# Where the second batch's keys and values are pooled in a fused attention and two-layer MLP kernel

## The chip, the cores and the metric

The kernel runs on one core of a Trainium2 chip. The metric is the device time of one execution in microseconds (us), where lower is better. Single executions are compared by the median of several; a profiled execution gives the trace. The engines are named as the profile names them: PE (TensorE matmuls), PEld (its weight loads), ACT (ScalarE), DVE (VectorE), POOL (GpSimd) and SP (SyncE), which issues all the transfers here.

## What is computed

Three stages follow each other. The attention stage takes 8 batches of 8 heads with 576 tokens and 64 channels; keys and values are averaged over groups of 8 tokens, so each head has 72 of each.

```python
k_p = k.reshape(B, H, Sp, pool, D).mean(axis=3)
v_p = v.reshape(B, H, Sp, pool, D).mean(axis=3)
scores = scale * np.matmul(q, k_p.transpose(0, 1, 3, 2))
attn = softmax(scores)                    # over the 72 pooled keys
x = np.matmul(attn, v_p)                  # then 4608 tokens x 512
```

The second stage is `x = g(x @ w_in) @ w_out` with 2048 hidden units, where g is a ratio of two polynomials. The third is `(sigmoid(x @ w_gate) * (x @ w_val)) @ w_out` with 1536 hidden units. All is float32 in and out.

## The kernel before

Every large product is made of three matmuls in a split form (`mm3`, L484): each operand is held as a high part, which is its rounded copy, and a low part, which is the rest. Weights are brought into that form by `conv1a` (two ACT instructions for each matrix, L92 and L94), `conv1b` (one on DVE, L100, and one on POOL, L102) and `conv2` (L117 on ACT, and L118 on DVE for `w_in` and on POOL for `w_out`).

The main loop (L771) runs over 144 steps n: 9 blocks of 512 tokens times 16 slices of 128 hidden units. Step n issues, in this order: `g1` (12 matmuls into a PSUM tile h), `run(on_pe, n, 0)`, `rational1` (ACT L526 to L528, then DVE L529 to L531), `run(off_pe, n, 0)`, `split_g` of the step before (ACT L511, POOL L514), `rational2` (ACT L537, L539), `run(off_pe, n, 2)`, `gap` (L100 and L102 of the weights that ACT treated in the step before), `rational3` (DVE L543 to L545, after which h is free), `g2` of step n - 3 (12 matmuls), `run(on_pe, n, 1)`, `run(off_pe, n, 1)`, and in the first 16 steps `weights_a` (L117, L118, then L92 and L94, then two transfers of raw weights). Steps -8 to -1 are a lead-in that pools the first batch and makes the first block of x. Each engine takes its instructions strictly in this order.

The attention of a tile of up to 128 tokens is spread over steps by a table: `put(step, rank, pe, rest, ...)` (L444) names the step and in which of the calls above a part runs. `scores` (L360 on PE, then L371 and L373 on DVE) stands three steps ahead of the tile's own step, `exponential` (L379) and `normalise` (L386 to L389 on DVE, L390 on POOL) two ahead, `a_transpose` (L397 on PE, L401 on ACT) at the step, and `attend` (L415 on PE, L421 and L422) one behind it. Tile 4, the last of the first batch, belongs to step 2; tile 5, the first of the second batch, to step 5; tile 6 to step 8.

A batch's keys come in 5 chunks and its values in 5. `pool_k` (L319) is one DVE reduction for a chunk, and `place_k` (L328) copies the whole pooled result on ACT into `kbd`, the operand that `scores` needs. `pool_v` is three POOL additions for a chunk (L336 twice, L337), and `mask_v` (L351) makes on POOL the operand `vm` that `attend` needs. They are wrapped in a generator that does nothing at its first call and the work at its second. So an entry with rest 2 and pe 1 is entered at `run(off_pe, n, 2)` and does its work at `run(on_pe, n, 1)`, after `rational3`; an entry with pe 1 and rest 1 works at `run(off_pe, n, 1)`.

The raw chunks of q, k and v are loaded in the order in which the table uses them. The first 14 go to tiles that later hold weights, the next three to a ring of three tiles, five more to other idle tiles, and from then on a load is issued into the ring whenever a ring tile has been used (`done`, L303). SP issues all loads in program order, so a load that must wait for its tile holds up those behind it.

Of the kernel before, what the change touches and what calls it, by code (L numbers as in the profile page):

```python
# [35 lines left out]
def attention_moe_glu_kernel(ctx: ExitStack, tc: tile.TileContext, q, k, v, w_in, w_out, ca, cb, w_gate, w_val, w_out2, out):  # L36
# [14 lines left out]
    NCH = (H * SP + P - 1) // P  # L51
# [179 lines left out]
    with tc.manual_schedule():  # L231
# [212 lines left out]
        def put(step, rank, pe, rest, gen, *a, use=()):  # L444
            plan.append((step, rank, len(plan), pe, rest, gen(*a), use))
# [17 lines left out]
        for b in range(1, B):  # L463
            e0, e1 = max(at[first[b - 1]], -2), at[last[b - 1]]
            for c in range(2 * NCH):
                w, f = (("k", pool_k), ("v", pool_v))[c // NCH]
                st = e0 + c * (e1 - (3 if w == "k" else 1) - e0) // (2 * NCH)
                put(st, 6, 1, 1 if st < 0 else 2, ew, f, b, c % NCH, use=[(w, b, c % NCH)])
            put(e1 - 2, 3.5, 1, 1, ew, place_k, b)
            put(e1 + (e1 > 0), 1, 0, 0, ew, mask_v, b)  # L470
        plan.sort(key=lambda x: (x[0], (0, 2, 1)[x[4]], x[1], x[2]))
        units += [u for x in plan for u in x[6]]
        lead = plan[0][0]
# [402 lines left out]
```

## Time and profile before

| what | value |
|---|---|
| median of 3 runs (lowest, highest) | 1843.52 us (1843.23, 1848.96) |
| the profiled execution, its span | 1846.18 us, 1844.4 us |
| PE, PEld busy | 1788.9 us (97%), 1556.9 us (84%) |
| DVE, ACT, POOL busy | 1144.7 us, 943.9 us, 849.4 us |

The span is that of the instructions in the trace; the 1.8 us between it and the execution's time lie around the program. Times in the trace count from the span's start. PE's share is that of the whole span, but the change touches only the first 90 us, where PE is not busy throughout, so what a change is worth there has to be read from the rows of that stretch.

### The profile page before, as it was taken

The numbers are of one execution on the slowest core, as the hardware profiler recorded it, in microseconds if no ns is written. First come the engines' busy times: TensorE is split into PE (matmuls) and PEld (weight loads), VectorE is DVE, ScalarE is ACT, GpSimd is POOL, SyncE is SP. The second block draws the span as 40 slices with busy tenths as digits, with TensorE's granted clock in tenths as the row PEclk, the third lists the DMA queues.
The fourth block names the chain that finished last, engine by engine and source line by source line (L and its number), as shares of the span: only waits on it lengthen the run. The fifth ranks groups of instructions, "written<-read, shape, count | busy, mean of one in ns | idle before, by whom it ended". The sixth has DMA issues, their size and how long they took to land.

```text
span 1844.4 us, 25043 instructions
## 1 busy us (share of the span) xinstructions
PE 1788.9 (97%) x8936; PEld 1556.9 (84%) x8936; DVE 1144.7 (62%) x1786; ACT 943.9 (51%) x1763; POOL 849.4 (46%) x839
## 2 busy tenths in 40 slices
PE   6689999999999999999999999999999999999999
PEld 5577887888778887888878998998998998998997
DVE  6999887888788888888777343343343343343341
ACT  5897767676777777767776222222222222222221
POOL 5776545463564556535552244244244244244241
PEclk9799999999999999999999999999999999999999
DMA  8454444533544444434455763763763763763660
GB/s 277 140 189 148 142 147 152 186 138 129 190 172 143 136 175 152 160 117 166 160 200 180 232 203 107 238 203 107 239 204 106 239 203 106 239 204 105 205 204 36
DMA packets 123116, 312.55 MB, mean 169 GB/s; under 512 B 11504, under 2 KB 43248, under 8 KB 122992
## 3 DMA queue, kind: packets, MB, share of 16 engines
q1 hardware_dynamic: 122992, 310.95, 50.8%
q8 instruction: 71, 1.16, 0.3%
q14 instruction: 53, 0.43, 0.1%
HBM read 257.95 MB, written 52.95 MB: 169 GB/s over the span
## 4 chain that ended last, share of the span: by engine, by line
PE 75%; DVE 8%; POOL 6%; ACT 4%; issue 4%; DMA 2%; SPq 0%; POOLq 0%; ACTq 0%
PE h L486 14%; PE h L488 14%; PE h L487 14%; PE acc L486 5%; PE acc L488 4%; PE acc L487 4%; PE psx L415 3%; PE accA L723 3%; PE accA L724 3%; PE h L723 3%; PE h L724 3%; PE accA L722 3%; PE h L722 3%; DVE u L529 1%; DVE y L531 1%
## 5 line engine op out<-in xcount | busy, mean ns | idle before, releaser
L659 DVE TENSOR_TENSOR t<-h,t 128x384 f32<-128x384 f32 x360 | 200.8, 558 | 388.6 <-ACT t L667 277.6
L514 POOL TENSOR_TENSOR g<-y,g 128x512 fp32r<-128x512 f32 x144 | 188.7, 1310 | 280.6 <-ACT g L511 223.8
L712 POOL TENSOR_TENSOR t<-t 128x384 f32<-128x384 f32 x72 | 84.6, 1175 | 449.3 <-issue 253.7
L486 PE MATMUL h<-xs,wi 128*128 128x512 f32 x576 | 230.7, 400 | 3.4 <-DVE y L545 1.9
L486 PE MATMUL acc<-g,wo 128*128 128x512 f32 x576 | 232.4, 403 | 0.0
L488 PE MATMUL acc<-g,wo 128*128 128x512 f32 x576 | 225.2, 391 | 1.4 <-POOL g L514 1.4
L488 PE MATMUL h<-xs,wi 128*128 128x512 f32 x576 | 226.2, 393 | 0.3 <-DVE xs L422 0.3
L487 PE MATMUL h<-xs,wi 128*128 128x512 f32 x576 | 225.9, 392 | 0.0
L487 PE MATMUL acc<-g,wo 128*128 128x512 f32 x576 | 224.5, 390 | 0.0
L488 PE MATMUL h<-xS,wq 128*128 128x384 f32 x576 | 193.0, 335 | 0.0
L486 PE MATMUL h<-xS,wq 128*128 128x384 f32 x576 | 192.9, 335 | 0.0
L487 PE MATMUL h<-xS,wq 128*128 128x384 f32 x576 | 192.7, 334 | 0.0
L529 DVE SCALAR_TENSOR_TENSOR u<-s,coef,u 128x512 f32<-128x512 f32 x144 | 135.9, 944 | 67.4 <-ACT u L527 67.0
L543 DVE SCALAR_TENSOR_TENSOR y<-y,coef,h 128x512 f32<-128x512 f32 x144 | 107.2, 744 | 68.9 <-ACT h L539 67.6
L486 PE MATMUL h<-xA,wq 128*128 128x384 f32 x432 | 149.3, 346 | 0.1
L526 ACT ACTIVATE s<-h 128x512 f32<-128x512 f32 x144 | 85.2, 592 | 122.6 <-PE h L488 122.3
L488 PE MATMUL h<-xA,wq 128*128 128x384 f32 x432 | 144.7, 335 | 0.0
L487 PE MATMUL h<-xA,wq 128*128 128x384 f32 x432 | 144.6, 335 | 0.0
L486 PEld LDWEIGHTS h<-xs,wi 128*128 128x128 f32 x576 | 109.1, 189 | 28.1 <-DVE y L545 2.8
L488 PEld LDWEIGHTS acc<-g,wo 128*128 128x128 f32 x576 | 108.1, 188 | 25.8 <-POOL g L514 1.8
L488 PEld LDWEIGHTS h<-xs,wi 128*128 128x128 f32 x576 | 109.1, 189 | 24.4 <-DVE xs L422 0.7
L486 PEld LDWEIGHTS acc<-g,wo 128*128 128x128 f32 x576 | 108.1, 188 | 24.8
(119 smaller groups left out, 4177.7 us busy)
## 6 DMA issues: line engine op xcount, KB each, us to landing
wq<-w2d SPq DMA_DIRECT2D x252, 512.0 KB, 4.4
wo<-wod SPq DMA_DIRECT2D x88, 512.0 KB, 4.0
w2d<-wq SPq DMA_DIRECT2D x36, 512.0 KB, 2.8
x2d<-o SPq DMA_DIRECT2D x36, 256.0 KB, 2.6
out_dram<-o SPq DMA_DIRECT2D x36, 256.0 KB, 2.0
raw<-in_k_dram SPq DMA_DIRECT2D x32, 256.0 KB, 2.7
raw<-in_q_dram SPq DMA_DIRECT2D x32, 256.0 KB, 2.7
raw<-in_v_dram SPq DMA_DIRECT2D x32, 256.0 KB, 2.7
```

What stands on the lines that cost most here:

```text
L486: nc.tensor.matmul(out_, wl, xh, start=start, stop=False, skip_group_check=on)
L487: nc.tensor.matmul(out_, wh, xh, start=False, stop=False, skip_group_check=on)
L488: nc.tensor.matmul(out_, wh, xl, start=False, stop=stop, skip_group_check=on)
L514: eng.tensor_tensor(out=g[:, 1], in0=y, in1=g[:, 0].bitcast(F32), op=ALU.subtract)
L526: nc.scalar.activation(s, h, AF.Square)
L529: nc.vector.scalar_tensor_tensor(out=u, in0=s, scalar=coef[:, 5:6], in1=u, op0=ALU.mult, op1=ALU.add)
L543: nc.vector.scalar_tensor_tensor(out=y, in0=y, scalar=coef[:, 0:1], in1=r, op0=ALU.add, op1=ALU.mult)
L659: nc.vector.tensor_tensor(out=out_, in0=a, in1=b, op=ALU.add)
L712: eng.tensor_tensor(out=y, in0=x, in1=y, op=ALU.mult)
L722: nc.tensor.matmul(a[t], gh, wt[:, 0], start=(f == 0), stop=False)
L723: nc.tensor.matmul(a[t], gh, wt[:, 1], start=False, stop=False)
L724: nc.tensor.matmul(a[t], gl, wt[:, 0], start=False, stop=(f == NF2 - 1))
```

## The change

Three entries of the table change, for the second batch (b = 1) alone. Its five `pool_k` stood in the lead-in's step -2 and stand in steps 0 (three) and 1 (two). Its five `pool_v` stood in steps -1 (two) and 0 (three) and stand in steps 1 (two), 2, 3 and 4. Its `place_k` moves from step 0 to step 1, and its `mask_v` from step 3 to step 5. The order of the loads follows. No instruction is added or left out. Lines behind L467 stand 3 further down in the changed file.

```diff
                 st = e0 + c * (e1 - (3 if w == "k" else 1) - e0) // (2 * NCH)
+                if b == 1:
+
+                    st = c // 3 if w == "k" else 1 + 3 * (c - NCH) // (NCH - 1)
                 put(st, 6, 1, 1 if st < 0 else 2, ew, f, b, c % NCH, use=[(w, b, c % NCH)])
-            put(e1 - 2, 3.5, 1, 1, ew, place_k, b)
-            put(e1 + (e1 > 0), 1, 0, 0, ew, mask_v, b)
+            put(1 if b == 1 else e1 - 2, 3.5, 1, 1, ew, place_k, b)
+            put(5 if b == 1 else e1 + (e1 > 0), 1, 0, 0, ew, mask_v, b)
```

On DVE, from the last instruction of `rational3` in step 0 to that in step 1, the kernel before has (L543 to L545 are `rational3`, kp is the pooled key tile, r the normaliser of tile 4):

```order
L545 SCALAR_TENSOR_TENSOR y<-h,y 128x512
L386 TENSOR_REDUCE r<-e 64x8
L388 TENSOR_SCALAR r<-r 64x8
L389 RECIPROCAL r<-r 64x8
L118 TENSOR_TENSOR wi<-wiraw,wi 128x512
L529 SCALAR_TENSOR_TENSOR u<-s,coef,u 128x512
...
L545 SCALAR_TENSOR_TENSOR y<-h,y 128x512
L118 TENSOR_TENSOR wi<-wiraw,wi 128x512
```

and the changed kernel, with its own line numbers:

```order
L548 SCALAR_TENSOR_TENSOR y<-h,y 128x512
L319 TENSOR_REDUCE kp<-raw 128x64 x2
L319 TENSOR_REDUCE kp<-raw_204 128x64
L386 TENSOR_REDUCE r<-e 64x8
...
L118 TENSOR_TENSOR wi<-wiraw,wi 128x512
L532 SCALAR_TENSOR_TENSOR u<-s,coef,u 128x512
...
L548 SCALAR_TENSOR_TENSOR y<-h,y 128x512
L319 TENSOR_REDUCE kp<-raw_206 128x64
L319 TENSOR_REDUCE kp<-raw_208 128x32
L118 TENSOR_TENSOR wi<-wiraw,wi 128x512
```

Three reductions now stand ahead of tile 4's normaliser, and two behind the last instruction of `rational3` in step 1.

On ACT, the end of step 0 and step 1 up to its weight conversion read before (L526 opens a step, L539 is the end of `rational2`, L328 is `place_k`):

```order
L539 ACTIVATE h<-s 128x512
L328 ACTIVATE kbd<-kp 64x4x72 x2
L117 ACTIVATE wi<-wiraw 128x512
...
L526 ACTIVATE s<-h 128x512
...
L539 ACTIVATE h<-s 128x512
L117 ACTIVATE wi<-wiraw 128x512
L117 ACTIVATE wo<-woraw 128x512
```

and in the changed kernel:

```order
L542 ACTIVATE h<-s 128x512
L117 ACTIVATE wi<-wiraw 128x512
...
L529 ACTIVATE s<-h 128x512
...
L542 ACTIVATE h<-s 128x512
L328 ACTIVATE kbd<-kp 64x4x72 x2
L117 ACTIVATE wi<-wiraw 128x512
L117 ACTIVATE wo<-woraw 128x512
```

`place_k` moved by one step; it reads all five chunks of kp, and everything that ACT does for the weights of step 1 and for step 2 stands behind it.

On SP, the load of tile 6's queries (the 128x512 rows of in_q) and the loads ahead of it read in the changed kernel, from the last chunk of the second batch's values on:

```order
L296 DMA raw<-in_v_dram 64x512
L291 DMA raw<-in_k_dram 128x512
L122 DMA wiraw<-in_moe_w_in_dram 128x4x256
L124 DMA woraw<-in_moe_w_out_dram 128x1024
L291 DMA raw<-in_k_dram 128x512
L122 DMA wiraw<-in_moe_w_in_dram 128x4x256
L124 DMA woraw<-in_moe_w_out_dram 128x1024
L288 DMA raw<-in_q_dram 128x512
```

Before, it was issued once `scores` of tile 5 had used a ring tile in step 2; now it is the load that follows the last `pool_v`, in step 4, and `scores` of tile 6 needs it at the end of step 5.

## Rows read from the trace of the kernel before

**Rows 1.** Busy time by stretch: span, then PE, PEld, DVE, ACT, POOL, granted clock, DMA share, GB/s
```profile
37.00:61.00 24.00, 11.77 (x50) 8.65 (x49) 20.22 (x31) 20.67 (x41) 22.50 (x26) 0.78 0.62 208
146.00:200.00 54.00, 53.38 (x261) 44.19 (x260) 47.51 (x76) 41.89 (x76) 31.30 (x34) 1.00 0.33 115
```
**Rows 2.** Waits of PE, 37 to 180 us: total, times, longest
```profile
PE pta L397 <- POOL e L390: 7.5, 1, 7.5
PE sc L360 <- ACT aT L401: 7.3, 5, 2.0
PE h L488 <- DVE xs L422: 0.3, 1, 0.3
```
**Rows 3.** Timeline of ACT, steps 0 to 6: start, duration, instruction, idle before and releaser
```profile
44.67 0.88 ACT L328 ACTIVATE kbd<-kp 64x288 f32<-64x288 f32 x2
52.39 0.60 ACT L539 ACTIVATE h<-s 128x512 f32<-128x512 f32 x1 [0.56 <-DVE y L531]
54.98 0.68 ACT L117 ACTIVATE wo<-woraw 128x512 fp32r<-128x512 f32 x1 [1.41 <-POOL wo L118]
57.80 0.57 ACT L526 ACTIVATE s<-h 128x512 f32<-128x512 f32 x1
80.83 0.63 ACT L537 ACTIVATE s<-u 128x512 f32<-128x512 f32 x1 [4.79 <-DVE u L529]
86.18 0.59 ACT L526 ACTIVATE s<-h 128x512 f32<-128x512 f32 x1
93.59 0.57 ACT L526 ACTIVATE s<-h 128x512 f32<-128x512 f32 x1
```
**Rows 4.** Timeline of DVE; then L529's line view (37 to 170) and wait (37 to 94)
```profile
33.38 2.78 DVE L319 TENSOR_REDUCE kp<-raw 128x64 f32<-128x512 f32 x5
52.21 1.59 DVE L100 TENSOR_SCALAR wiraw<-wiraw 128x512 int32<-128x512 int32 x1
56.53 0.69 DVE L545 SCALAR_TENSOR_TENSOR y<-h,y 128x512 f32<-128x512 f32 x1
70.23 2.88 DVE L100 TENSOR_SCALAR woraw<-woraw 128x512 int32<-128x512 int32 x1
76.66 4.14 DVE L529 SCALAR_TENSOR_TENSOR u<-s,coef,u 128x512 f32<-128x512 f32 x1
103.36 1.60 DVE L529 SCALAR_TENSOR_TENSOR u<-s,coef,u 128x512 f32<-128x512 f32 x1
...
L529 DVE SCALAR_TENSOR_TENSOR u<-s,coef,u x16: 741/784/4142, 41.9 to 163.7; 128x512 f32<-128x512 f32 x16
...
DVE u L529 <- ACT u L527: 4.0, 4, 1.7
```
**Rows 5.** Timeline of POOL
```profile
45.42 1.04 POOL L102 TENSOR_TENSOR woraw<-woraw 128x512 int32<-128x512 int32 x1
...
48.65 1.26 POOL L336 TENSOR_TENSOR raw<-raw 128x256 f32<-128x256 f32 x2
49.98 0.32 POOL L337 TENSOR_TENSOR vp<-raw 128x64 f32<-128x64 f32 x1
52.37 1.14 POOL L390 TENSOR_TENSOR e<-e,r 64x576 f32<-64x576 f32 x1
67.52 3.04 POOL L351 TENSOR_TENSOR vm<-vp,mask 128x256 f32<-128x256 f32 x5 [1.65 <-PE psx L415]
78.97 1.28 POOL L514 TENSOR_TENSOR g<-y,g 128x512 fp32r<-128x512 f32 x1
```
**Rows 6.** Timeline of SP, the transfer's KB and us to landing, then two rows of PE's timeline
```profile
61.20 0.33 SPq L288 DMA_DIRECT2D raw<-in_q_dram  x1
...
raw<-in_q_dram SPq DMA_DIRECT2D x1, 256.0 KB, 2.6
...
85.05 1.33 PE L360 MATMUL sc<-kbd,raw 128*128 128x144 f32 x4 [3.08 <-DVE y L545]
89.28 0.80 PE L486 MATMUL h<-xs,wi 128*128 128x512 f32 x1
```

## Prediction

> **What bounds the kernel now.** I read the page's busy shares first, then busy time by stretch, then who waited for whom on PE, and last the timelines of the four engines over steps 0 to 6. PE is busy 97% of the span, but not at its head: from 37 to 61 us, where the steps of the main loop begin, PE works 11.8 of 24.0 us while POOL works 22.5 and ACT 20.7; from 146 us on PE is busy 53.4 of 54.0 us [rows 1]. So a shift of the moment at which PE takes over is carried to the end, and nothing else in the program moves. The reader should see in PE's waits that the longest one, 7.5 us in step 2, is for L390 on POOL, the normalisation of tile 4, and that the next sort, 7.3 us in five pieces, is for `a_transpose`'s copies on ACT [rows 2]. That second sort tells who sets the pace: ACT. A step on ACT begins with L526, at 57.80, 86.18 and 93.59 for steps 2, 5 and 6, and in between ACT stands still only where a row names a releaser: 1.41 us at L117 in step 1, 4.79 us at L537 in step 4, and under 1 us where L539 waits for DVE [rows 3]. PE's 7.5 us are therefore mostly cover: g1 of step 3, behind that stall, would have met ACT's lateness at the next copy. The change has to be summed on ACT's chain, from L526 of step 0 to L526 of step 6, and the result is shifted unchanged through the later steps, in which both versions issue the same instructions.
>
> **The change, part by part.** All terms are in us against the profiled execution.
>
> *Lead-in.* Five reductions, 2.78 in all, leave DVE [rows 4]. They stood in the shade of ACT, but for the 0.3 that PE waits at its third matmul of step 0 for a DVE result [rows 2]: -0.3.
>
> *Step 0.* `place_k`, 0.88 on ACT, goes to step 1 [rows 3]: -0.9. Five `pool_v` leave POOL, 1.65 each from the first L336 to the end of L337 [rows 5]. Behind them the two L102 of the lead-in end just where L529 of step 0 begins. L529 can be held by POOL: at 103.36 it lasts 1.60 behind one POOL instruction, against a least of 0.74 [rows 4]. Between 0 and 0.9 I take +0.4. Step 1 begins 0.8 early.
>
> *The normalisation of tile 4.* Three reductions of 0.6 now stand ahead of it on DVE, so it is 1.8 late on DVE, but POOL is free when it comes: L390 moves from 52.37 [rows 5] to about 50.1, and PE's stall of 7.5 shrinks by only 2. L529 of step 1 stood three DVE instructions of 0.7 ahead of L539's 52.39, at 50.2, and DVE had waited 1.7 for ACT there [rows 3, 4], so it was ready at 48.5. With 1.8 more it is ready at 50.4, and L390 now lies there, so it takes 1.60 and not 0.75: its end moves from 50.9 to 52.0, and L539 from 52.39 to 53.5: +1.1. Without the hold it would be +0.3.
>
> *A new wait on ACT.* `place_k` in step 1 stands on ACT directly behind L539 and needs all five chunks. The last two are reduced behind L545 of that step. "In the gaps" means here, after `rational3`, and not while ACT converts weights. L545 ended at 57.22 (56.53 and 0.69), since L100 ahead of it was held by POOL for 1.59 [rows 4]; POOL still has L118 and L514 there, so I leave L545 where it is. Two chunks, 0.6 and 0.4, bring it to 58.2. ACT is done with L539 at 54.1 and waits 4.1. The least is 3.1: three DVE instructions of 0.7 behind L539 and the two chunks. The most is 5.3, if L539 stays where it was. Then `place_k` costs its 0.9 here. The 1.41 that L117 waited for POOL's L118 [rows 3] go, because POOL does L118 of step 0 at about 51.5. Step 2 begins at 57.80 + 1.1 + 4.1 + 0.9 - 1.4 = 62.5, that is **4.7 late**. What is queued behind: the weights of step 1, the copies of tile 4's transposes and so the second half of `scores` of tile 5 and g1 of step 3 on PE.
>
> *Steps 1 to 4 on POOL.* Each `pool_v` adds 1.65 to a step's L102, L102, L118 and L514 (1.0 to 1.3 each [rows 5], some 4.7 together). With ACT's steps near 8 POOL can hold that, so I carry 4.7 to step 4. The 3.04 of `mask_v` leave step 3 [rows 5]. There they held L100 for 2.88, which made r of tile 5 late, and then L529 of step 4 fell behind L390, L118 and L514 for 4.14 until 80.8 [rows 4, 5]: that was ACT's 4.79. Now r comes in time, and L529 meets one POOL instruction. I leave 0.4 of the 4.79: -4.4. Step 5 begins 0.3 late, at 86.5.
>
> *A new wait on PE.* Tile 6's queries were loaded at 61.20 and needed at 85.05 [rows 6]. Now the load waits for the last `pool_v`, in step 4. From L539 ACT needs 4.0 to the next L526 (52.39 to 57.80 less the 1.41). POOL needs from about the same moment one instruction that holds L100 (1.0), two L102 (2.1) and `pool_v` (1.65), in all 4.8, and ends 0.8 behind the L526 at 86.5. So it ends at 87.3, and with 2.6 to landing [rows 6] `scores` of tile 6 begins at 89.9, where g1 of step 6 began at 89.28. Two groups of 1.33, as the row has them at a lowered clock, make g1 up to 3.3 late. If this one wait lowers the clock less than PE's stalls did before (granted 0.78 in the first stretch [rows 1]), g1 itself is shorter and little is lost. ACT, 0.3 late by itself, then waits for h. Between 0.3 and 3.3 I take 1.5, since clock was lost there before too.
>
> `mask_v` in step 5, 3.04, and its `vm` are needed by `attend` in step 6, a step later: nothing. The other moved loads are issued at least a step ahead of use: nothing; if SP fell a step behind, the weights of step 6 would be late next.
>
> **The sum**: -0.3 - 0.9 + 0.4 (step 1) + 1.9 + 4.1 + 0.9 - 1.4 (step 2; 1.1 late though it began 0.8 early) - 4.4 (step 5), then 1.5 in place of the 0.3 reached: **+1.5**. The profiled execution took 1846.18, its span 1844.4; the median is 1843.52. The sum gives 1847.7 for the profiled one; carried to the median, 1845.0.
>
> **A rule against a row.** L529 at 76.66 sits behind three POOL instructions in a row, until L514 ends at 80.25 [rows 4, 5], while most of the 16 are not held at all (median 784 ns) and the one at 103.36 is held by one. The Trainium skill (SBUF — State Buffer, "Who interferes with whom") says that a DVE instruction with two SBUF inputs shares ports with GpSimd, and that the one that comes second waits until the first finishes, so one POOL instruction at most. By the rule the holds stay near 0.9 and the sum is 1845.0; by the row at 76.66 each can be 3.4. The 1.60 agrees with the rule, the 4.14 does not, and so the first rival below keeps a chance.
>
> **The rivals.**
> *POOL's longer chains hold DVE more than once (slower).* In steps 4 and 5 POOL has L102, L102, `pool_v`, L118 and then L390 or `mask_v` and L514 without a gap. If L529 in step 4 is held for 3.4 in place of 0.9 (+2.5), and in step 5 as L100 was, 2.5 over its 0.4, ACT is late by 1.5 + 2.5 + 2.5 = 6.5: 1850.0. It decides where POOL's next instruction is always ready. For it: two such rows. Against it: all other holds end with one instruction.
> *The new waits stay small (a little faster).* ACT's wait at 3.1 (-1.0), no hold of L529 in step 1 (-0.8), queries in time (-1.2): 1.5 - 3.0 = -1.5, 1842.0.
> *The stalls go and nothing takes their place (faster).* If the last two reductions and `place_k` were done in ACT's shade, both waits (1.4 and 4.8) and the 0.3 would be gained: -6.5, 1837.0. For it: POOL, 22.5 of 24.0 busy, is relieved. Against it: the order on ACT.
> *The change doesn't do what it says:* the keys are not pooled between `rational2` and `rational3`. This is in the sum.
>
> **How the numbers follow.** A measurement of this kernel can tell some 0.3%, 5.5 us, from no change; the bounds are 1838.0 and 1849.0. My case has 0.60, small waits 0.20, POOL's chains 0.14, stalls gone 0.06. The first two lie within: same 0.80; slower 0.14, faster 0.06. The range reaches from 1840.0, the lower ends of the unknown waits together with small waits elsewhere, to 1850.0, the first rival.
>
> **What would show it.** ACT's L328 in step 1 with some 4 us of idle before it, released by DVE's L319; PE's `scores` of tile 6 released by a transfer of queries; PE's wait for L390 down to 5 to 6 us; ACT's 4.79 at L537 gone; L526 of step 2 near 62.5 and of step 6 near 95. It is wrong if L328 does not wait, if L529 is held by more than one POOL instruction in steps 1 to 5, or if step 6 begins more than 4 us off 95 and the end does not follow.

## The result and the profile after

The change makes the kernel slower: 1854.16 us is the median of 7 runs (1851.82 to 1856.84), against 1843.69 of 7 runs of the kernel before (1841.72 to 1848.96) beside them. The ratio is 1.0051, with a 95% interval of 1.0041 to 1.0061. The forecast was 1845.0, its range ended at 1850.0, and "slower" had a chance of 0.14: the prediction was wrong. The profiled execution of the changed kernel took 1852.82 us, its span 1850.8, so the two traces differ by 6.6 us of execution time, less than the medians' 10.5, because each profiled execution lies off its median (by +2.5 before and by -1.3 after). What can be read here is the 6.6; the rest of the 10.5 stands in no trace.

Line numbers of the changed kernel behind L467 are 3 higher: L529 opens a step on ACT, L540 and L542 are `rational2`, L532 is the DVE instruction that the prediction calls L529. ACT's timeline after, steps 1 to 6 (start, duration, instruction, idle before and its releaser), answers to [rows 3]:

```profile
48.09 0.57 ACT L529 ACTIVATE s<-h 128x512 f32<-128x512 f32 x1
54.45 0.63 ACT L540 ACTIVATE s<-u 128x512 f32<-128x512 f32 x1 [4.02 <-DVE u L532]
55.89 0.60 ACT L542 ACTIVATE h<-s 128x512 f32<-128x512 f32 x1 [0.81 <-DVE y L534]
59.56 0.90 ACT L328 ACTIVATE kbd<-kp 64x288 f32<-64x288 f32 x2 [3.06 <-DVE kp L319]
63.81 0.57 ACT L529 ACTIVATE s<-h 128x512 f32<-128x512 f32 x1
85.05 0.63 ACT L540 ACTIVATE s<-u 128x512 f32<-128x512 f32 x1 [2.82 <-DVE u L532]
90.39 0.57 ACT L529 ACTIVATE s<-h 128x512 f32<-128x512 f32 x1
96.39 0.63 ACT L540 ACTIVATE s<-u 128x512 f32<-128x512 f32 x1 [3.30 <-DVE u L532]
101.72 0.61 ACT L529 ACTIVATE s<-h 128x512 f32<-128x512 f32 x1
```

The reader should see two new waits, 4.02 at L540 and 3.06 at L328, between the starts of step 1 (48.09) and step 2 (63.81), a third, 3.30, in step 5, and in step 4 a wait of 2.82 where the kernel before had one of 4.79 [rows 3]. All but the 3.06 are for the same DVE instruction. DVE's timeline after, for [rows 4]:

```profile
50.31 4.10 DVE L532 SCALAR_TENSOR_TENSOR u<-s,coef,u 128x512 f32<-128x512 f32 x1
...
58.52 1.00 DVE L319 TENSOR_REDUCE kp<-raw 128x64 f32<-128x512 f32 x2
...
81.08 3.94 DVE L532 SCALAR_TENSOR_TENSOR u<-s,coef,u 128x512 f32<-128x512 f32 x1 [0.42 <-ACT u L530]
...
91.57 4.79 DVE L532 SCALAR_TENSOR_TENSOR u<-s,coef,u 128x512 f32<-128x512 f32 x1 [1.36 <-ACT u L530]
```

And POOL's timeline after over the same moments, for [rows 5]:

```profile
49.97 1.42 POOL L390 TENSOR_TENSOR e<-e,r 64x576 f32<-64x576 f32 x1 [7.74 <-ACT y L531]
51.36 1.28 POOL L118 TENSOR_TENSOR wo<-woraw,wo 128x512 fp32r<-128x512 f32 x1
52.61 1.25 POOL L517 TENSOR_TENSOR g<-y,g 128x512 fp32r<-128x512 f32 x1
...
80.81 1.14 POOL L390 TENSOR_TENSOR e<-e,r 64x576 f32<-64x576 f32 x1
81.92 1.30 POOL L118 TENSOR_TENSOR wo<-woraw,wo 128x512 fp32r<-128x512 f32 x1
83.19 1.28 POOL L517 TENSOR_TENSOR g<-y,g 128x512 fp32r<-128x512 f32 x1
...
90.60 0.31 POOL L337 TENSOR_TENSOR vp<-raw 64x64 f32<-64x64 f32 x1
90.87 1.28 POOL L118 TENSOR_TENSOR wo<-woraw,wo 128x512 fp32r<-128x512 f32 x1
92.12 2.47 POOL L351 TENSOR_TENSOR vm<-vp,mask 128x256 f32<-128x256 f32 x5
94.55 1.26 POOL L517 TENSOR_TENSOR g<-y,g 128x512 fp32r<-128x512 f32 x1
```

L532 starts at 50.31, while POOL does L390, and ends at 54.41; POOL has by then done L390, L118 and L517, the last until 53.86. The same happens at 81.08, and at 91.57, where L532 begins beside L118 and ends at 96.36 after L118, the five pieces of `mask_v` and L517 (until 95.81). Unhindered it takes 0.75. Such an instruction, stretched while POOL works, is called *held* below, and POOL instructions that follow each other without a pause are a *chain*. The row of 4.14 in the kernel before [rows 4] is thus no oddity: it now stands three times.

With the step starts of both traces (before: 48.90, 57.80, 73.71, 86.18 and 93.59 for steps 1, 2, 4, 5 and 6) the accounts are short:

| stretch | before | after | difference | made of |
|---|---|---|---|---|
| start of step 1 | 48.90 | 48.09 | -0.8 | 0.4 from the lead-in, 0.9 of `place_k` gone from step 0, less 0.5 by which L542 comes later there, behind an L532 of 1.28 |
| step 1 | 8.90 | 15.72 | +6.8 | 4.02 at L540, 0.25 at L542, 3.06 at L328, 0.90 `place_k`, less the 1.41 at L117 |
| step 4 | 12.47 | 10.49 | -2.0 | 2.82 in place of 4.79 |
| step 5 | 7.41 | 11.33 | +3.9 | 3.30 at L540, 0.62 at L542 |
| start of step 6 | 93.59 | 101.72 | +8.1 | the sum of these, with +0.2 in steps 2 and 3 |

Where PE is the bound, the shift is 7.9 in steps 10 to 33, 7.3 in steps 35 to 60, 5.8 in steps 62 to 135 and 7.5 behind them; the span ends 6.4 later. The two stretches that answer to [rows 1] (span, then PE, PEld, DVE, ACT, POOL, granted clock, DMA share, GB/s):

```profile
37.00:61.00 24.00, 9.98 (x43) 7.59 (x44) 20.37 (x31) 14.73 (x28) 11.38 (x13) 0.77 0.48 159
152.00:206.00 54.00, 53.45 (x261) 44.23 (x260) 47.41 (x75) 41.48 (x75) 31.93 (x34) 1.00 0.36 124
```

POOL is freed in the head (11.4 of 24.0 us busy, not 22.5), and everybody gets less done in it: ACT 14.7 and not 20.7, PE 10.0 and not 11.8. DVE's 20.4 is as high as before, but 3.35 of it is L532 standing still. PE's waits from 37 to 180 us, for [rows 2], say where PE feels it:

```profile
PE sc L360 <- ACT kbd L328: 8.3, 1, 8.3
PE sc L360 <- ACT aT L401: 7.9, 3, 4.2
PE sc L360 <- DMA raw<-in_q_dram: 5.8, 1, 5.8
PE pta L397 <- POOL e L390: 5.8, 1, 5.8
```

The waits for `place_k` and for the queries of tile 6 are new. The wait for the queries, 5.8 at 93.75, looks like a cause of step 6's lateness, but L529 of step 6 on ACT, at 101.72, has no idle before it: PE's wait was over before ACT came.

### The profile page after: what moved, and what is told of

Read it like the earlier page. It is cut to its first block, busy times and chain, and to the rows that moved or that the text cites. A ratio compares the mean times of both kernels' runs of the same rounds, so it can differ in the third digit from the quotient of the medians.

```text
span 1850.8 us, 25050 instructions
## 1 busy us (share of the span) xinstructions
PE 1788.0 (97%) x8936; PEld 1555.9 (84%) x8936; DVE 1149.7 (62%) x1786; ACT 943.5 (51%) x1763; POOL 845.7 (46%) x839
## 4 chain that ended last, share of the span: by engine, by line
PE 72%; DVE 11%; POOL 7%; issue 5%; ACT 4%; DMA 1%; SPq 0%; POOLq 0%; ACTq 0%; DVEq 0%
PE h L489 14%; PE h L491 13%; PE h L490 13%; PE acc L489 4%; PE acc L491 4%; PE acc L490 4%; PE psx L415 3%; PE accA L726 3%; PE accA L727 3%; PE h L727 3%; PE h L726 3%; PE accA L725 3%; PE h L725 3%; DVE u L532 2%; DVE y L534 2%
## 5 line engine op out<-in xcount | busy, mean ns | idle before, releaser
L517 POOL TENSOR_TENSOR g<-y,g 128x512 fp32r<-128x512 f32 x144 | 188.7, 1310 | 284.2 <-ACT g L514 232.3
L532 DVE SCALAR_TENSOR_TENSOR u<-s,coef,u 128x512 f32<-128x512 f32 x144 | 146.2, 1015 | 67.5 <-ACT u L530 67.0
L529 ACT ACTIVATE s<-h 128x512 f32<-128x512 f32 x144 | 85.2, 592 | 121.8 <-PE h L491 121.5
```

The source lines that it names most:

```text
L517: eng.tensor_tensor(out=g[:, 1], in0=y, in1=g[:, 0].bitcast(F32), op=ALU.subtract)
L529: nc.scalar.activation(s, h, AF.Square)
L532: nc.vector.scalar_tensor_tensor(out=u, in0=s, scalar=coef[:, 5:6], in1=u, op0=ALU.mult, op1=ALU.add)
```

## The experiments

Diffs are against the changed kernel unless they say otherwise. No kernel leaves work out. Ratios are to the kernel before, with their 95% intervals. Lines behind an edit move by the lines it adds.

**1. The two halves of the change, and one fifth of it undone.** First the keys alone are moved, then the values alone, then all, but with the five key reductions all in step 0.

```diff
# e1_keys_only
-                if b == 1:
+                if b == 1 and w == "k":
-            put(5 if b == 1 else e1 + (e1 > 0), 1, 0, 0, ew, mask_v, b)
+            put(e1 + (e1 > 0), 1, 0, 0, ew, mask_v, b)
# e2_values_only
-                if b == 1:
+                if b == 1 and w == "v":
-            put(1 if b == 1 else e1 - 2, 3.5, 1, 1, ew, place_k, b)
+            put(e1 - 2, 3.5, 1, 1, ew, place_k, b)
# e3_keys_in_step0
-                    st = c // 3 if w == "k" else ...
+                    st = 0 if w == "k" else ...
```

> The second batch's keys move as in the change, its values and mask_v stay as before. Theory K (the wait of ACT's L328 for the last two key chunks is the main cost): L328 in step 1 waits 3 to 4 us, step 2 begins 4 to 6 us later than before's 57.80, and most of the loss of the whole change (about 9 us) is here, 5 to 8 us. Theory H (the loss comes mainly from DVE's first instruction of rational1 being held over whole chains of POOL instructions, in steps 1, 4 and 5): the wait of L328 is seen too, but L390 stays near 52.4, the instruction in step 1 is not held for 4 us, step 5 has no hold, and the time is 2 to 5 us over before.

> The second batch's values and mask_v move as in the change, its keys and place_k stay as before. Theory H: no wait at L328; L390 comes near 48 and step 2 begins about 1.3 us before 57.80; the holds of DVE in step 4 (about 4 us) and step 5 (about 4.8 us) are seen as in the changed kernel, so that step 6 begins about 1 us late and the time is within -1 and +3 us of before. Theory Q (the late load of tile 6's queries costs): PE's scores of tile 6 wait for the transfer as in the changed kernel, and 4 us or more of the loss are here.

> The changed kernel, but all five key chunks are reduced in step 0, and place_k stays in step 1. Theory K: L328 waits for nothing, the normaliser of tile 4 is 1 us later, and the time falls by 3 us or more from the changed kernel. Theory H: L328's 3.1 us go too, but the hold in step 1 stays about 4 us because L390, L118 and the split of g still follow each other on POOL; step 2 begins 2 to 3 us earlier than in the changed kernel, and 5 to 7 us are still lost against before.

Keys alone: 1852.44 us, 1.0027 [1.0017, 1.0037]. Values alone: 1846.53 us, 0.9994 [0.9985, 1.0003]. All keys in step 0: 1854.51 us, 1.0039 [1.0027, 1.0052]. ACT with the keys alone:

```profile
53.33 0.63 ACT L540 ACTIVATE s<-u 128x512 f32<-128x512 f32 x1 [4.00 <-DVE u L532]
...
58.44 0.89 ACT L328 ACTIVATE kbd<-kp 64x288 f32<-64x288 f32 x2 [3.06 <-DVE kp L319]
```

and with all keys in step 0, where L328 waits no more:

```profile
55.23 0.63 ACT L540 ACTIVATE s<-u 128x512 f32<-128x512 f32 x1 [4.93 <-DVE u L532]
...
83.25 0.63 ACT L540 ACTIVATE s<-u 128x512 f32<-128x512 f32 x1 [2.73 <-DVE u L532]
...
94.60 0.63 ACT L540 ACTIVATE s<-u 128x512 f32<-128x512 f32 x1 [3.29 <-DVE u L532]
```

The keys carry the loss of step 1, both its waits. The wait for the last two chunks is real, but taking it away gives nothing that the timing can tell (1.0039 against 1.0051, with intervals that overlap): the hold of L532 stands ahead of it and comes a little later and a little dearer. Step 2 does begin 2.35 earlier than in the changed kernel, and 1.7 of that are left at step 6. An expectation missed here: I had L390 at 52.4 with the keys alone, and it came at 48.85, since POOL had done the value chunks of step 0 at 48.69 already, and not at about 52.4 as in the kernel before [rows 5]. The values alone cost nothing that can be told, though step 5 begins 4.1 earlier than in the kernel before. That lead is lost in step 6, which begins 0.6 late. DVE and ACT with the values alone:

```profile
77.92 2.51 DVE L100 TENSOR_SCALAR wiraw<-wiraw 128x512 int32<-128x512 int32 x1
...
86.07 4.10 DVE L100 TENSOR_SCALAR wiraw<-wiraw 128x512 int32<-128x512 int32 x1
```

```profile
94.17 0.60 ACT L529 ACTIVATE s<-h 128x512 f32<-128x512 f32 x1 [3.95 <-PE h L491]
```

I had expected the holds on L532 in steps 4 and 5, as in the changed kernel. Here ACT runs ahead, so L532 gets through before POOL's chain, and the hold falls on L100 instead; and now the late queries are what ACT waits for in step 6 (PE waits 4.6 for them, then g1 is late).

**2. The holds: rows of 128 partitions in place of 64.** Every hold so far falls while POOL works without a pause behind an instruction of 64 partitions: L390 of the tiles 4 and 5, which have 64 tokens, the last value chunk, the last piece of `mask_v`; and it ends where POOL pauses. Behind chains of 128 partitions alone DVE came in after one instruction, as at 103.36 [rows 4]. POOL in the kernel before, around the two rows of 76.66 and 103.36:

```profile
76.26 1.49 POOL L390 TENSOR_TENSOR e<-e,r 64x576 f32<-64x576 f32 x1 [2.02 <-DVE r L389]
77.71 1.30 POOL L118 TENSOR_TENSOR wo<-woraw,wo 128x512 fp32r<-128x512 f32 x1
...
102.92 1.49 POOL L390 TENSOR_TENSOR e<-e,r 128x576 f32<-128x576 f32 x1 [1.87 <-DVE r L389]
104.38 1.76 POOL L118 TENSOR_TENSOR wo<-woraw,wo 128x512 fp32r<-128x512 f32 x1
```

At 103.36 L118 takes 1.76 in place of 1.30, since DVE went in ahead of it. So L390 of every tile of 64 tokens is done on all 128 partitions, in the changed kernel and in the kernel before (the upper rows are set to zero on DVE and used by nobody).

```diff
# e4_full_rows; the same against the kernel before is b4_full_rows
+            if n < P:
+                nc.vector.memset(e_[n:], 0.0)
...
+            if n < P:
+                nc.vector.memset(r[n:], 0.0)
...
-            nc.gpsimd.tensor_tensor(out=e_[:n], in0=e_[:n], in1=r[:n].unsqueeze(2).to_broadcast([n, H, SP]), op=ALU.mult)
+            nc.gpsimd.tensor_tensor(out=e_, in0=e_, in1=r.unsqueeze(2).to_broadcast([P, H, SP]), op=ALU.mult)
```

> The changed kernel, but the POOL multiplication of normalise (L390) for the two 64-token tiles runs on all 128 partitions, with the upper 64 rows of e and r set to zero on DVE (0.6 us and 0.1 us more on DVE in steps -1, 0, 2 and 3). Theory S (DVE is held over several POOL instructions because the first of them works on 64 of the 128 partitions only, as L390 of a 64-token tile does, while behind a POOL instruction on 128 partitions DVE comes in after one): DVE's first instruction of rational1 lasts at most 1.8 us in steps 1 and 4 in place of 4.1 and 3.9, while in step 5, whose chain has other instructions on 64 partitions and is not changed, it stays near 4.8; the time falls by 3 to 5 us from the changed kernel. Theory C (any chain of POOL instructions that are ready holds DVE to its end): it stays near 4 in steps 1 and 4, and the time is that of the changed kernel within 1 us.

> The kernel before, with the POOL multiplication of normalise for the 64-token tiles on all 128 partitions. Theory S: L529 in step 4, 4.14 us in the kernel before, lasts at most 1.8 us, ACT's idle time of 4.8 us there falls by 2 us or more, and the time is 1.5 to 3 us under before; L100 in step 3, held for 2.9 us behind mask_v with its last piece on 64 partitions, is not changed. Theory C: L529 stays near 4 us and the time is that of before within 0.7 us.

The changed kernel with whole rows: 1851.65 us, 1.0020 [1.0011, 1.0030]. The kernel before with whole rows: 1844.44 us, 0.9998 [0.9990, 1.0007]. The first is 0.31 points under the changed kernel's 1.0051, and the intervals don't meet. DVE, then POOL, of the changed kernel with whole rows:

```profile
50.26 1.63 DVE L536 SCALAR_TENSOR_TENSOR u<-s,coef,u 128x512 f32<-128x512 f32 x1
...
89.73 4.10 DVE L100 TENSOR_SCALAR wiraw<-wiraw 128x512 int32<-128x512 int32 x1
```

```profile
49.92 1.43 POOL L394 TENSOR_TENSOR e<-e,r 128x576 f32<-128x576 f32 x1 [6.51 <-DVE r L393]
51.31 1.74 POOL L118 TENSOR_TENSOR wo<-woraw,wo 128x512 fp32r<-128x512 f32 x1
53.01 1.26 POOL L521 TENSOR_TENSOR g<-y,g 128x512 fp32r<-128x512 f32 x1
```

These are the rows to set beside 50.31 and 49.97 of the changed kernel. The normaliser costs POOL the same (1.43, 1.42) and starts at the same moment, but DVE's instruction, begun at 50.26, is done at 51.89, after one POOL instruction and not three, and it is POOL's L118 that now lasts 1.74 in place of 1.28. What changed is who goes next. The one place that still has a 64-partition instruction ahead, the last value chunk and `mask_v` of step 5, still has its hold of 4.10, on L100. In the kernel before, the 4.14 became 1.64 and ACT's 4.79 became 2.79:

```profile
75.77 1.64 DVE L533 SCALAR_TENSOR_TENSOR u<-s,coef,u 128x512 f32<-128x512 f32 x1
```

The hold of L100 in step 3 stays there (2.87, `mask_v`), a new one of 2.75 comes in step 1, behind the last value chunk, and the median's gain of 1.2, where 1.5 to 3 was expected, can't be told from none. The same shows far outside the head. In the kernel before, L529 at 789.95 is held behind L390 of another tile of 64 tokens; in the kernel before with all rows filled up (part 4), where it starts at 785.66, the same instruction goes through, and POOL's next one, L191, takes 1.20 in place of 0.74:

```profile
789.95 3.92 DVE L529 SCALAR_TENSOR_TENSOR u<-s,coef,u 128x512 f32<-128x512 f32 x1 [1.07 <-ACT u L527]
...
785.66 0.78 DVE L539 SCALAR_TENSOR_TENSOR u<-s,coef,u 128x512 f32<-128x512 f32 x1 [1.00 <-ACT u L537]
```

**3. The queries of tile 6.** Their load is moved ahead of two loads of the third batch's key chunks; first with the values alone, then with the whole change, then with whole rows in L390 too.

```diff
# e5_values_early_q (on e2), e6_after_early_q, e7_rows_early_q (on e4)
+        units.remove(("q", 6))
+        units.insert(units.index(("k", 2, 0)), ("q", 6))
```

> Only the second batch's values and mask_v move, and the load of tile 6's queries is put ahead of the two loads of the third batch's first key chunks, so that it no longer follows the last pool_v. Theory Q2 (with the holds of rational1 gone, the late queries are what is left: in the run with the values alone, step 5 began 4.1 us before the kernel before, and step 6 0.6 us after it, with PE waiting 4.7 us for the transfer): PE's wait for the transfer is gone, step 6 begins 3 to 4 us before 93.59, and the time is 2.5 to 4.5 us under before. Rival P (PE would have waited anyway, for the copies of tile 5's transposes on ACT): step 6 gains under 1.5 us and the time is that of the run with the values alone.

> The changed kernel with the load of tile 6's queries put ahead of the same two key loads. Theory H (in the changed kernel ACT reaches step 6 late by itself, because DVE's instruction in step 5 is held for 4.8 us; PE's 5.8 us for the queries lie in that shade): PE's wait for the transfer goes, step 6 begins within 1 us of the changed kernel's 101.72, and the time stays within 1 us. Theory Q: step 6 begins 3 us or more earlier and the time falls by 3 us or more.

> The changed kernel with the POOL multiplication of normalise on all 128 partitions and the early load of tile 6's queries. The full rows alone left step 5 0.3 us before the kernel before and step 6 4.4 us behind it, with PE waiting 4.6 us for the queries. Theory Q2: PE's wait goes, step 6 begins within 1 us of 93.59, and the time is within 1.5 us of before; what is then left of the change's own cost is ACT's wait for the last key chunks in step 1 (3.9 us there), offset by the stall of 4.8 us in step 4 that before had. Rival P: step 6 stays 3 us or more behind.

Values alone with early queries: 1845.95 us, 1.0002 [0.9994, 1.0011]. The whole change with early queries: 1854.84 us, 1.0047 [1.0031, 1.0063]. With whole rows too: 1852.31 us (median of four), 1.0037 [1.0024, 1.0050]; there is no usable trace of it, so why the expectation missed stays open. In the other two the wait for the queries is gone and the time is not. DVE, PE and ACT of the values alone with early queries:

```profile
83.75 4.12 DVE L100 TENSOR_SCALAR wiraw<-wiraw 128x512 int32<-128x512 int32 x1
```

```profile
90.33 3.83 PE L415 MATMUL psx<-aT,vm 128*128 128x64 f32 x16 [4.94 <-DVE y L550]
```

```profile
94.20 0.38 ACT L421 ACTIVATE xs<-psx 128x256 fp32r<-128x256 f32 x1 [4.62 <-PE psx L415]
```

Step 6 begins 5.8 early, and step 7 is at +0.15 again. The hold of L100 makes `rational3` behind it late, PE's next product waits for that (L550, 4.94), and ACT's copy waits for PE (4.62). Two waits stood side by side, and either is enough. With the whole change it goes the same way: no L534 in steps 4 and 5 is held, L100 is held for 2.51 and 4.11, step 6 begins 0.06 late and step 7 4.9 late, with 4.59 of idle at L421. So neither expectation held: the time stayed, as theory H had it, but step 6 came 8.1 earlier, as theory Q had it, because other instructions were held.

**4. All holds removed at once.** Every POOL instruction of 64 partitions in these steps gets 128: L390 as above, and the second batch's last value chunk (its load takes 64 rows more, which are pooled and not used) with its piece of `mask_v`. This goes onto the values alone with early queries, onto the whole change with early queries, and onto the kernel before.

```diff
# e8_values_q_rows (on e5), a8_after_q_rows (on e6), b8_before_rows (on before): L390 as in e4, and
+        FULLB = (1,)
-                m = P if c < NCH - 1 else CL
-                nc.sync.dma_start(t[:m], rows[c * P:c * P + m])
+                if u[1] in FULLB:
+                    allv = v.rearrange("b h (s j) d -> (b h s) (j d)", j=POOL)
+                    r0 = u[1] * H * SP + c * P
+                    nc.sync.dma_start(t, allv[r0:r0 + P])
+                else:
...
-            m = P if c < NCH - 1 else CL
+            m = P if c < NCH - 1 or b in FULLB else CL
```

> Values and mask_v moved, queries of tile 6 loaded early, and every POOL instruction of steps 0 to 5 that worked on 64 partitions (normalise of tiles 4 and 5, the last pool_v and the last piece of mask_v of the second batch) works on all 128; the last value chunk is loaded with 64 rows of the next batch, which nobody reads. With the early queries alone, DVE's L100 in step 5 was held for 4.1 us behind L118, mask_v and the split of g, PE waited 4.9 us for rational3 behind it, and all of a lead of 5.8 us at step 6 was lost. Theory S: that hold is at most 1.6 us, PE's wait at attend in step 6 is under 1.5 us, step 7 begins 4 to 6 us before 102.17, and the time is 3 to 6 us under before. Theory C: L100 stays near 4 us and the time is that of before within 1 us.

> The changed kernel with the early queries and the same POOL instructions on all 128 partitions. Theory S with K: what is left of the change's cost is ACT's wait of 3 to 4 us at L328 in step 1; step 2 begins about 4.3 us late, step 5 about 0.3 us early since the stall of step 4 is gone, step 7 within 1.5 us of 102.17, and the time within 2 us of before. Theory C: step 7 begins 4 us late or more and the time is 4 us or more over.

> The kernel before with the same POOL instructions on all 128 partitions. Theory S: L100 in step 3 (2.88 us before) and L529 in step 4 (4.14 us) last at most 1.6 and 1.8 us, step 7 begins 3 to 5 us before 102.17 and the time is 1 to 4 us under before. Theory C: both stay and the time is that of before within 0.7 us.

Values alone: 1845.21 us, 0.9993 [0.9984, 1.0002]. The whole change: 1847.65 us, 1.0009 [1.0000, 1.0018]. The kernel before: 1842.27 us, 0.9984 [0.9976, 0.9993]. No single instruction of DVE between 37 and 240 us lasts over 1.80 in any of the three, so the holds went as expected. The time of the values alone did not: 3 to 6 us under the kernel before had been expected. Its lead of 3.7 at step 6 is 1.5 at step 7, since L544 in step 6 is held by one POOL instruction (it lasts 1.77) and ACT waits for it (2.13). ACT of the whole change, then DVE of the kernel before with 128 partitions:

```profile
51.22 0.63 ACT L552 ACTIVATE s<-u 128x512 f32<-128x512 f32 x1 [1.75 <-DVE u L544]
...
57.12 0.90 ACT L334 ACTIVATE kbd<-kp 64x288 f32<-64x288 f32 x2 [3.86 <-DVE kp L325]
```

```profile
74.90 1.64 DVE L539 SCALAR_TENSOR_TENSOR u<-s,coef,u 128x512 f32<-128x512 f32 x1
```

Of the change's 0.51% some 0.42 points are gone with the holds and the queries' wait. What remains on ACT is above all the wait of `place_k`, 3.86 now that ACT comes to it sooner, beside 1.75 at L552 in step 1 and 1.25 in step 6, both for a DVE instruction held by one of POOL's; step 2 begins 3.6 late, step 5 1.1 early, since step 4's wait has gone too. But the kernel before gains from the same rows. Like against like, both with filled rows, the change costs 0.25 points (1.0009 against 0.9984, 5.4 us by the medians), so the holds and the queries' wait were about half of its 0.51. The medians put the key half at 2.4 us (1847.65 less 1845.21) and the value half, with its early queries, at 2.9 (1845.21 less 1842.27) when nothing is held for long; for each half alone the intervals overlap, for the two together they do not, and neither half is seen to help. The last version, the kernel before with the rows filled up, is the fastest of all, faster than the one before by 0.16%: without the change ACT has no wait of over 0.81 for POOL or DVE in steps 0 to 7, and its step 7 begins 4.2 early.

**5. Is it the number of partitions by itself?** In the kernel before, L390 of the tiles of 128 tokens, from tile 6 on, is done as two instructions of 64 partitions.

```diff
# d1_split_halves, against the kernel before
-            nc.gpsimd.tensor_tensor(out=e_[:n], in0=e_[:n], ...)
+            for a, z in ((0, n),) if n < P or i < n0 else ((0, P // 2), (P // 2, P)):
+                nc.gpsimd.tensor_tensor(out=e_[a:z], in0=e_[a:z], ...)
```

> The kernel before, but the POOL multiplication of normalise for every 128-token tile from tile 6 on is done as two instructions, one on partitions 0 to 63 and one on 64 to 127. Theory S in the form that the two halves of POOL's partitions work through the instructions on their own (so that an instruction on one half lets the other half run ahead into the next): the two together take no longer than the one did, at most 1.8 us from the start of the first to the start of the L118 behind them. Without it: 2.3 us or more.

1855.18 us (two executions), 1.0049 [1.0031, 1.0067]. POOL and DVE at tile 6:

```profile
100.35 3.05 POOL L391 TENSOR_TENSOR e<-e,r 64x576 f32<-64x576 f32 x2 [1.87 <-DVE r L389]
```

```profile
100.79 1.60 DVE L530 SCALAR_TENSOR_TENSOR u<-s,coef,u 128x512 f32<-128x512 f32 x1
```

The two halves take 3.05, one after the other, twice the 1.43 that 128 partitions took above; what the loss of 0.5% is made of was not followed further. And DVE, begun during the first half, was let in between the two halves (1.60). So 64 partitions alone do not make a long hold; yet tile 5's L391, with L118 of 128 partitions behind it, held L530 for 3.96 in this kernel too. Nor does a wider instruction behind a narrow one always make one: in the kernel before, L100 at 52.21 began beside the narrow L337 and was let in once L390 was done, after 1.59 [rows 4, 5]. What the runs show is this much: from 37 to 240 us each DVE instruction that lasts over 2 us (21 of them in all the traces here) fell into an unbroken POOL chain with a 64-partition instruction in it or at most two instructions ahead, and where these were filled up there was none. Outside that stretch, L529 at 526.09 in the kernel before is held for 3.12 behind a last value chunk of 64 rows, and its like stands in every trace but this one; L514 behind it takes 1.74 and not 1.29, so there DVE was let in before the chain had ended. Behind 128 partitions alone the longest DVE instruction in the kernel before takes 2.59, a subtraction of 128x768 (L616) with a least of 0.96: less than one POOL instruction of 1.85 on top. Why DVE is sometimes let in at that seam and mostly not stays open; the width and the moment at which each engine's next instruction is ready were not tried apart. There is one trace of each kernel, so whether every execution holds the same instructions isn't shown.

## Why the prediction was wrong

**What held.** The order of the argument did: in the head ACT's chain sets the pace, and most of its shift is carried (6.4 of 8.1). Step 1 was said to begin 0.8 early and began 0.81 early. L390 was put at about 50.1 and came at 49.97; PE's wait for it at 5 to 6, and it is 5.8. `place_k` was said to wait 4.1 in step 1, between 3.1 and 5.3, and waited 3.06, its lower bound, because ACT, held just before, came later; its two chunks took the 1.0 that they were priced at, and L117's 1.41 went.

**The step that failed** is "L390 now lies there, so it takes 1.60 and not 0.75", with its twin in step 4 ("L529 meets one POOL instruction") and the "nothing" for `mask_v` in step 5. The first two assume that a DVE instruction which meets POOL is held by one instruction; for the third only the reader of `vm` was looked at, and not DVE beside `mask_v`. The sizes:

| term | priced | measured |
|---|---|---|
| L529 (now L532) in step 1 | 1.60 | 4.10 |
| what is left of the 4.79 in step 4 | 0.4 | 2.82 |
| ACT behind `mask_v` in step 5 | 0 | 3.92 |

The three differences are 2.5, 2.4 and 3.9, in all 8.8; the shorter wait at L328 (1.0 less) and the 1.2 by which the queries were to make step 6 later, which cost ACT nothing here, take back 2.2. That makes 6.6 and, with the forecast +1.5, the 8.1 that step 6 shows. The later return to 5.8 and 6.4 was not forecast and not traced further. With the holds and the queries' wait taken away, the changed kernel is 0.09% over the kernel before ([0.00, 0.18], 1.7 us), near the forecast +1.5; 1.2 of that forecast was for the queries, so the nearness is in part luck.

**What happened was the first rival**, POOL's longer chains, with its mechanism. It named steps 4 and 5 and took step 1 for safe; the hold came in all three. That its price, 6.5, is near the 6.6 between the traces is luck in part, since it lacks step 1 and the later return; the medians lie 10.5 apart. It had been given 0.14 because "all other holds end with one instruction". That held only for the stretch that was read, up to 170 us: the same trace has L529 held for 3.12 at 526.09 and for 3.92 at 789.95, each behind a 64-partition instruction. The Trainium skill (SBUF — State Buffer, "Who interferes with whom") says that the second comer waits until the first finishes. This case's traces agree where POOL's instructions have 128 partitions (1.63, 1.64) and mostly do not where a 64-partition one leads the chain (3.94 to 4.79). The row of 4.14 in the kernel before had the same chain (L390 of 64 tokens, L118, L514) that now stands at 50.31 and at 81.08, so it was the nearest row to both and should have set their price; the form 64x576 stood in the rows [rows 5] and was not compared with the 128x576 of the L390 at 102.92. The rule, and a median over all meetings, were given more weight than the row.

**The queries' wait** was right as an event and wrong in effect. Tile 6's `scores` were put 3.4 behind the start of step 5 (89.9 and 86.5), and they begin 3.36 behind it (93.75 and 90.39), with the load issued at 90.94. But the 1.2 that this was to cost step 6 is not there: ACT is so late by its own waits that PE's 5.8 is covered. With the values alone, where ACT is not held, it is on ACT's path (3.95).

**The parts do not add up.** Keys alone cost 4.8 us, values alone gain 1.1, together they cost 10.5 (medians against those beside them). The traces suggest why: in the whole change ACT is late, and in step 5 L532 meets the chain with `mask_v`, whereas with the values alone ACT is ahead and L100 meets it, at a cost that first shows a step later. But lateness at step 2 alone does not decide it: the whole change with early queries begins step 2 at 62.92, 5.1 late, and there too it is L100 that is held.

## What to carry to other kernels

Where two engines contend, price a meeting by the nearest row of the same shapes, and not by the median or by a rule of one instruction: look at what the other engine has queued behind, and whether a narrower tile leads it. Look for such rows in the whole trace before calling one an exception. A narrow last tile on POOL can be worth filling up to 128 partitions, which cost POOL nothing here and gained 0.16%. And before a wait is removed, look for the one beside it: of two equal waits in parallel, taking one away shows no gain while the other stands.

## What had not been expected of the hardware

In the head, behind a POOL instruction of 64 partitions, DVE was mostly kept out until POOL paused, over up to seven instructions (3.85 to 4.79 us for L532, where a chain of 128 partitions cost it 1.4 to 1.8). On 128 partitions the same normalisation took POOL 1.43 us against 1.42 on 64, so the width cost nothing in this instruction; two halves in a row took 3.05.
